# Block-causal attention with a SoLU feed-forward layer on one core: placing order by halves, loads shared by two pairs, W_out's rows permuted, and probabilities by way of DRAM for every second pair

## The chip, the cores and the metric

The kernel runs on one core of one Trainium2 chip, as one launch. The metric is the device time of that launch in microseconds (us). Before the change it is 729.7 us, the median of three runs (728.79 to 730.06).

A core has five engines with a program each. PE (TensorE) multiplies matrices, DVE (VectorE), ACT (ScalarE) and POOL (GpSimd) do elementwise work and reductions, and SP (SyncE) computes nothing: here it issues nearly all DMAs, one after the other. Each engine works through its own list of instructions in order. The DMAs themselves run on 16 DMA engines beside all of that.

## The reference

Eight batches of eight heads, 576 tokens, head size 64; then a feed-forward layer over all 4608 tokens:

```python
scores = scale * np.matmul(q, k.transpose(0, 1, 3, 2))      # scale = 1/8
mask = block_i >= block_j                                   # blocks of 64 tokens
attn = exp(scores - max) / (sum + 1e-09)
attn_out = np.matmul(attn, v)
x = attn_out.transpose(0, 2, 1, 3).reshape(4608, 512)
h = x @ w_in                                                # 512 -> 1024
sm = softmax(h); solu = h * sm
ln = (solu - mean) / sqrt(var + 1e-06) * g_ln
out = ln @ w_out                                            # 1024 -> 512
```

The weights w_in, w_out and g_ln arrive as 64-bit floats, q, k and v as 32-bit floats.

## The kernel before, in words

**Units of work.** Attention runs over 32 *pairs* p of heads (8 batches, 4 pairs each; heads 2hp and 2hp+1 in the two halves of the 128 partitions). The feed-forward layer, called MoE in the code, runs over 36 *tiles* t of 128 tokens. A tile can start when the four pairs of its batch are done. Products are made exact enough by splitting each operand in a high and a low part (names ending in h and l: `kh`, `kl`, `xh`, `xl`, `wih`, `wil`, `ch`, `cl`) and adding three matmul products.

**The order of the work** is not the order of the code. Every step is recorded by `op(engine, duration, function, ...)` with what it reads and writes, a key, and sometimes other engines that can do it (`alts`). `Schedule.run` (L109) then simulates all engines with these durations, always starting the ready step with the smallest key, and the instructions are issued in that order. The keys come from the table `PARAMS` (L41). An alternative engine is only open if its value there is under 3 (L79). A step of SP may have a `dma` time, which holds a simulated DMA channel, and a `tail` until its data have landed. At run time the engines keep this fixed order and wait for each other by semaphores.

**A pair** (function `attention`, L406). Pairs 0 to 3 transpose by PE; they are left out of what follows, as are the names with the ending 32.
1. `load` (L417) brings k and q into `kz` and `qz`: four DMAs each (L432), laid out so that DVE can transpose within blocks of 32 by 32. `loadv` (L439) brings v by three (L441, L445).
2. DVE transposes `kz` into `kt`, `qz` into `qt` (L474). ACT makes `kh`, `qh` (L475), POOL or DVE the low parts `kl` (L480, L481) and `ql` (L478). POOL casts the last 64 columns (L485).
3. PE computes the scores in PSUM (L515; the last block, L509). DVE masks and takes the row maximum (L536, L540); ACT takes the exponential into the probability buffer `pb` with row sums (L552).
4. DVE makes the reciprocals (L562, L563); POOL or ACT scales the probabilities (L570, L572). DVE transposes `pb` in place within blocks of 32 by 32 in two steps (L579).
5. `place` (L581) finishes the transposition by moving blocks between the quarters of the partitions: 16 DMAs, each 32 partitions of `pb` to 32 partitions of `pt` (L584):

```python
for r_ in range(4):
    for a_ in range(4):
        SP.dma_start(pt_[32 * r_ : 32 * r_ + 32, a_, :, :], pb[32 * a_ : 32 * a_ + 32, r_, :, :])
```

6. PE multiplies with v (`avmm`, L594: 52 matmul instructions at L596), ACT copies the result to `xt` (L395). `pb`, `pt` and `vr` have two buffers each; `kz`, `qz`, `kt`, `qt`, `kh` and the like have one.

**A tile** (function `moe`, L633). `xh` and `xl` (L648, L652), 24 matmuls with W_in (L673), row maximum (L679), exponential (L680), product (L681), then centring of `u` by the mean, on POOL or DVE (L683, L684), the square for the variance (L685). For tiles 4 to 34 (`PET <= t < PEL`) the centred tile is transposed by DVE into `zb` (L703), stored to a DRAM buffer `zd` (L704) and read back as `ct` (L705); ACT, POOL or DVE make `ch` (L711 to L713) and `cl` (L714, L715). Tiles 0 to 3 and 35 transpose by PE (L721, L724, L725). Then come 24 matmuls with W_out (L733), scaling (L737) and the store of the output (L739).

**Weights.** `prep` (L341) converts 16 pieces of weights at the start, one load each (L345), with `zb`, `ct` and `ob` as scratch space. L368 loads g.

Of the kernel before, what the change touches and what calls it, by code (L numbers as in the profile page):

```python
# [58 lines left out]
class Schedule:  # L59
# [49 lines left out]
    def run(self):  # L109
# [20 lines left out]
        while events:  # L130
# [18 lines left out]
            for e in engs:  # L149
# [46 lines left out]
                if best.dma > 0.0:  # L196
                    done = dmafree = max(done, dmafree) + best.dma
# [9 lines left out]
def kernel(  # L207
# [43 lines left out]
    qz, kz, qt, kt = (sb(x, [S]) for x in ("qz", "kz", "qt", "kt"))  # L251
# [87 lines left out]
    wkeys = []

    def prep(i, src, hi, lo, gcol, name, key):  # L341
# [3 lines left out]
        op("SP", 640, lambda: SP.dma_start(raw, src), w=[kr_], key=key, tail=2700, dma=1270)  # L345
# [60 lines left out]
    def attention(p):  # L406
# [7 lines left out]
        pep = p in PEP  # L414
        for nm, src, dst in (("kz", k, kz), ("qz", q, qz)):

            def load(nm=nm, src=src, dst=dst):  # L417
# [1 line left out]
                if peq:
                    for h in range(2):  # L420
                        dma.dma_start(
                            dst[:, 0:512].rearrange("p (c d) -> p c d", c=4)[:, :, 64 * h : 64 * h + 64],
                            src[b0, 2 * hp + h, 0:512, :].rearrange("(c p) d -> p c d", p=P),
                        )
                    r0 = 0 if nm == "kz" else 64
# [155 lines left out]
        def place():  # L581
            for r_ in range(4):
                for a_ in range(4):
                    SP.dma_start(pt_[32 * r_ : 32 * r_ + 32, a_, :, :], pb[32 * a_ : 32 * a_ + 32, r_, :, :])  # L584
# [199 lines left out]
```

## Time and profile before

| | |
|---|---|
| three runs | 728.79, 729.7, 730.06 us |
| profiled execution | 730.28 us |
| its span, first to last instruction | 728.5 us |
| mean granted clock of PE | 0.97 |
| moved by DMA | 125.49 MB, mean 172 GB/s |

The profile is of one execution. *Busy* is the time in which an engine has an instruction in work; PE's matmuls overlap, so a busy PE is not always at its peak. The stretches between busy times are idle, and a wait is put down to what ended it. In the profile's lines, "L596 PE MATMUL ps<-pt,vr" is line 596 of the kernel, the engine, the operation, and what it writes and reads; "SPq" is SP issuing a DMA, which is the time for issuing and not for moving data. The granted clock is 1.00 at full speed. The DMA share is the mean busy share of the 16 DMA engines.

### The profile page before, as it was taken

Reading aid. Unit: us, or ns where it says so; the run is one execution under the profiler, and the core shown is the slowest. Engines: PE = TensorE matmul, PEld = TensorE weight load, DVE = VectorE, ACT = ScalarE, POOL = GpSimd, SP = SyncE. Lnnn points to the kernel's source line nnn. Section 1 sums busy time; section 2 is a strip of 40 time slices with the busy share of each in tenths; the row PEclk is TensorE's granted clock in tenths of the full one; section 3 lists DMA queues with packets and bytes.
Section 4 is the critical chain, followed back from the end, with each engine's and each line's share of the span. In section 5 each row is a group of like instructions: output and inputs, shape, how many; then the busy total and the mean of one; then the engine's idle time right before and its main releaser. Section 6 shows DMA issues by size and latency. Waiting matters only on the chain.

```text
span 728.5 us, 14348 instructions
## 1 busy us (share of the span) xinstructions
PE 671.1 (92%) x4543; PEld 528.1 (72%) x4543; DVE 607.4 (83%) x1262; ACT 495.3 (68%) x1265; POOL 322.5 (44%) x491
## 2 busy tenths in 40 slices
PE   7786968999999998999999999899899988999997
PEld 6566757777677776778777777677677766878886
DVE  6999999988888999789799888899888789755672
ACT  5989958877777777665777686578585658434342
POOL 3755744454444655244353654245454434214310
PEclk7899989999999999999999999999999999999999
DMA  9584676676788888888778888888787874543431
GB/s 236 130 175 118 150 178 117 126 170 146 161 201 201 205 196 193 198 192 210 182 193 197 203 196 173 190 199 196 193 209 178 190 197 110 170 151 130 145 131 57
DMA packets 231547, 125.49 MB, mean 172 GB/s; under 512 B 190640, under 2 KB 206512, under 8 KB 231472
## 3 DMA queue, kind: packets, MB, share of 16 engines
q1 hardware_dynamic: 230416, 124.32, 70.1%
q8 instruction: 36, 0.59, 0.4%
q10 hardware_dynamic: 1056, 0.26, 0.2%
q14 instruction: 39, 0.32, 0.2%
HBM read 52.96 MB, written 25.69 MB: 108 GB/s over the span
## 4 chain that ended last, share of the span: by engine, by line
PE 32%; DVE 23%; SPq 14%; DMA 12%; ACT 12%; issue 5%; POOL 1%; DVEq 0%; ACTq 0%; POOLq 0%
PE ps L733 12%; SPq L584 11%; PE ps L673 9%; PE ps L596 5%; DVE pb L579 5%; DVE nm L540 5%; DMA pt<-pb 4%; ACT pb L552 4%; PE ps L515 4%; DMA ct<-zd 3%; ACT pb L572 3%; SPq L432 2%; DVE ub L681 2%; DVE zb L703 2%; PE ps L509 1%
## 5 line engine op out<-in xcount | busy, mean ns | idle before, releaser
L552 ACT ACTIVATE pb<-ps,nm 128x384 f32<-128x384 f32 (+4 forms) x288 | 157.3, 561 | 69.6 <-DVE nm L540 54.2
L540 DVE TENSOR_REDUCE nm<-ps 128x1 f32<-128x384 f32 (+4 forms) x288 | 131.8, 506 | 0.3
L596 PE MATMUL ps<-pt,vr 128*64 128x128 f32 (+2 forms) x1664 | 104.3, 286 | 25.4 <-DMA pt<-pb 13.7
L596 PEld LDWEIGHTS ps<-pt,vr 128*64 128x64 f32 x1664 | 90.2, 146 | 46.9 <-issue 16.4
L572 ACT ACTIVATE pb<-pb,rz 128x128 f32<-128x128 f32 (+4 forms) x191 | 101.2, 595 | 25.4 <-DVE rz L563 23.0
L579 DVE STREAM_TRANSPOSE pb<-pb 128x1536 f32<-128x1536 f32 (+1 forms) x56 | 102.1, 1829 | 9.5 <-POOL pb L570 5.8
L570 POOL TENSOR_SCALAR pb<-pb,rz 128x384 f32<-128x384 f32 (+4 forms) x97 | 62.3, 652 | 71.3 <-DVE rz L563 30.4
L733 PE MATMUL ps<-woh,ch 128*128 128x512 f32 x288 | 81.6, 405 | 4.0 <-ACT pb L552 3.4
L673 PE MATMUL ps<-wih,xh 128*128 128x512 f32 x288 | 83.8, 413 | 0.2 <-ACT xh L648 0.2
L673 PE MATMUL ps<-wil,xh 128*128 128x512 f32 x288 | 79.4, 398 | 0.0
L733 PE MATMUL ps<-woh,cl 128*128 128x512 f32 x288 | 78.7, 395 | 0.0
L673 PE MATMUL ps<-wih,xl 128*128 128x512 f32 x288 | 78.6, 395 | 0.0
L733 PE MATMUL ps<-wol,ch 128*128 128x512 f32 x288 | 78.6, 394 | 0.0
L733 PEld LDWEIGHTS ps<-woh,ch 128*128 128x128 f32 x288 | 51.8, 188 | 20.2 <-ACT pb L552 5.6
L703 DVE STREAM_TRANSPOSE zb<-ub 128x1024 f32<-128x1024 f32 x31 | 62.5, 2017 | 2.6 <-POOL ub L683 1.4
L673 PEld LDWEIGHTS ps<-wil,xh 128*128 128x128 f32 x288 | 54.8, 190 | 13.0
L673 PEld LDWEIGHTS ps<-wih,xh 128*128 128x128 f32 x288 | 51.1, 190 | 17.3 <-issue 4.8
L673 PEld LDWEIGHTS ps<-wih,xl 128*128 128x128 f32 x288 | 54.3, 188 | 12.8
L733 PEld LDWEIGHTS ps<-woh,cl 128*128 128x128 f32 x288 | 54.3, 188 | 12.8
L515 PE MATMUL ps<-kh,qh 64*128 64x384 f32 (+3 forms) x256 | 57.8, 390 | 6.2 <-ACT pb L552 1.8
L733 PEld LDWEIGHTS ps<-wol,ch 128*128 128x128 f32 x288 | 54.2, 188 | 12.7
L712 POOL TENSOR_SCALAR ch<-ct 128x512 fp32r<-128x512 f32 x36 | 22.0, 620 | 90.0 <-DMA ct<-zd 77.0
(116 smaller groups left out, 1262.3 us busy)
## 6 DMA issues: line engine op xcount, KB each, us to landing
pt<-pb SPq DMA_DIRECT2D x448, 100.0 KB, 2.2
zd<-zb SPq DMA_DIRECT2D x31, 512.0 KB, 3.0
ct<-zd SPq DMA_DIRECT2D x31, 512.0 KB, 4.3
out_dram<-ob SPq DMA_DIRECT2D x36, 256.0 KB, 3.1
vr<-in_v_dram SPq DMA_DIRECT2D x64, 128.0 KB, 3.3
kz<-in_k_dram SPq DMA_DIRECT2D x112, 72.0 KB, 2.7
qz<-in_q_dram SPq DMA_DIRECT2D x112, 72.0 KB, 3.0
ub<-in_moe_w_in_dram SPq DMA_DIRECT2D x8, 512.0 KB, 4.2
```

The costliest lines, as they stand in the source:

```text
L515: PE.matmul(PS(sps[h])[:, off : off + 128 * (i_ + 1)], w_[half[h], 128 * i_ : 128 * i_ + 128], x_[half[h], 0 : 128 * (i_ + 1)], start=n_ = ...
L540: op("DVE", t_dve(wid[u]), lambda sp=sp, off=off, u=u: DVE.tensor_reduce(out=nm_[u], in_=PS(sp)[:, off : off + wid[u]], axis=AX.X, op=ALU. ...
L552: ACT.activation(dst, src, AF.Exp, bias=nm_[u], accum_out=z_[zg][:, zc : zc + 1])
L570: op("POOL", 0.836 * nn + 243, lambda b=b, zg=zg, zc=zc: POOL.tensor_scalar(out=puv(pb, b, pep), in0=puv(pb, b, pep), scalar1=rz_[zg][:, z ...
L572: ("ACT", t_act(nn, 93), lambda b=b, zg=zg, zc=zc: ACT.activation(puv(pb, b, pep), puv(pb, b, pep), AF.Copy, scale=rz_[zg][:, zc : zc + 1] ...
L579: op("DVE", 1.058 * 128 * (s1 - s0) + 86, lambda s0=s0, s1=s1: DVE.transpose(pb[:, :, s0:s1, :], pb[:, :, s0:s1, :]), r=[("P", i, b) for b ...
L584: SP.dma_start(pt_[32 * r_ : 32 * r_ + 32, a_, :, :], pb[32 * a_ : 32 * a_ + 32, r_, :, :])
L596: PE.matmul(dst(PS(av)[half[h]]), vt[:, j, 64 * h : 64 * h + 64], pt_[:, a0:a1, sl, :], start=start, stop=stop)
L673: PE.matmul(o_, a_[:, c, :], w_[:, c, s_], start=(si == 0 and c == 0), stop=(si == 2 and c == NKI - 1))
L703: op("DVE", t_dve(DFF), lambda: DVE.transpose(zb.rearrange("p (r c i) -> p r c i", r=4, i=32), u.rearrange("p (c i r) -> p r c i", r=4, i= ...
L712: alts=[("POOL", 671, lambda c_=c_, h_=h_: POOL.tensor_scalar(out=h_, in0=c_, scalar1=1.0, scalar2=1.0, op0=ALU.mult, op1=ALU.mult), K["a_ ...
L733: PE.matmul(o_, a_[:, c, :], w_[:, c, :], start=(hf == 0 and si == 0 and c == 0), stop=(hf == 1 and si == 2 and c == 7))
```

## The change

**Pairs of heads.** A pair now holds heads ha and ha + 2, with `ha = 4 * (hp // 2) + zs` and `zs = p % 2`; the rows of W_in are loaded in the matching order, two DMAs a piece.

**Shared loads.** `kz` and `qz` get room for two pairs. From pair 4 on, every second pair issues four DMAs each for k and q that bring both pairs' data (`load2`). `kt` and `qt` are gone: DVE transposes in place, and the high and low parts read `kz` and `qz`.

**Placing.** For odd pairs the 16 DMAs go out in another order, by halves of the partitions. For pairs 4, 6, ..., 30 (`DRP`) one DMA stores the whole `pb` in a DRAM buffer `pd`, and four DMAs, after a wait for it, read `pt` from there.

**W_out's rows.** Row c\*128 + r\*32 + j of W_out (and of g) goes to partition 4j + r instead of 32r + j, by four DMAs a piece. L703 then reads 32 elements in a row where it read every fourth. Tiles 0 to 3 and 35, which transpose by PE, write the centred tile to `zb` in the permuted order; the first of them waits for all prepared weights, since `zb` is scratch space for these.

**Planner.** New durations for some steps, a DMA time of 5500 for `place` where it was 250, a limit on how far SP runs ahead of the DMAs (`DEPTH`), and a new table `PARAMS`. By it some alternatives close (centring on DVE, `ch` on POOL, `cl` on POOL, `xl` on DVE, scaling on ACT for pairs 0 to 3) and some open (the low part of the weights on POOL, the copies of kh and qh on DVE for pairs 0 to 3).

```diff
+DRP = tuple(range(4, 32, 2))
+PDMA = 5500
+DEPTH = 2500.0
-    "a_w": 189.2, "a_xh": -137.2, "a_xl": -269.8, "a_c": -179.5, "a_o": 359.2, "np": 32, "l0": -21.1,
+    "e1": 446.7, "e2": 16.2, "a_sp": 326.6, "a_sp32": 396.9, "a_lf": -295.5, "a_w": -763.6, "a_xh": 157.7,
+    "a_xl": 109.8, "a_c": 397.1, "a_o": 107.1, "np": 32, "l0": 36.7, "a_cl": -50.3, "a_ai": -221.8,
+    "aff": -308.3, "a_t3": -99.5, "a_cm": -493.3, "a_cg": 75.0, "a_sa": -235.7, "a_sa32": 555.4, "a_qh": 43.1,
+    "a_kl": -230.6, "a_ch": 260.5, "a_chd": 58.4, "a_clo": 184.7, "ct0": -293.1,
...
-                    done = dmafree = max(done, dmafree) + best.dma
+                    dmafree = max(t + min(best.dur, 600.0), dmafree) + best.dma
+                    engfree[e] = max(done, dmafree - DEPTH)
+                    done = max(engfree[e], dmafree)
...
-    qz, kz, qt, kt = (sb(x, [S]) for x in ("qz", "kz", "qt", "kt"))
+    qz, kz = (sb(x, [2, S]) for x in ("qz", "kz"))
+    pd = [dp.tile([P, 4, NSL * 32], F32, name=f"pd{i}") for i in range(2)]
...
-    w_in_w = w_in.bitcast(U32).rearrange("(c p) (n t) -> p c n t", p=P, t=2)
-    w_out_w = w_out.bitcast(U32).rearrange("(c p) (n t) -> p c n t", p=P, t=2)
+    w_in_w = w_in.bitcast(U32).rearrange("(a h z d) (n t) -> d a z h n t", h=2, z=2, d=64, t=2)
+    w_out_w = w_out.bitcast(U32).rearrange("(c r j) (n t) -> r j c n t", r=4, j=32, t=2)
+    def rows(dst, src):
+        for r_ in range(4):
+            SP.dma_start(dst[r_::4], src[r_])
+    def heads(dst, src):
+        for h in range(2):
+            SP.dma_start(dst[64 * h : 64 * h + 64], src[:, h])
...
+        zs = p % 2
+        ha = 4 * (hp // 2) + zs
+            def load2(nm=nm, src=src, dst=dst):
+                for g in range(4):
+                    SP.dma_start(
+                        dst[32 * g : 32 * g + 32].rearrange("p m (g d) -> p (m g) d", d=32),
+                        src[b0, ha + g - g % 2 : ha + g - g % 2 + 2, :, 32 * (g % 2) : 32 * (g % 2) + 32].rearrange("m (g p) d -> p (m g) d", p=32),
+                    )
+            elif zs == 0:
+                op("SP", 2600, load2, w=[(nm, 0), (nm, 1)], key=lk, tail=1700, dma=3740)
...
-            op("DVE", t_dve(S) + 30, lambda z=z, t=t: DVE.transpose(t, z), r=[x + "z"], w=[x + "t"], key=kk)
+            op("DVE", t_dve(S) + 30, lambda z=z: DVE.transpose(z, z), r=[zk], w=[zk], key=kk)
...
-            for r_ in range(4):
-                for a_ in range(4):
+            for d_ in (2, 3, 0, 1):
+                for a_ in (0, 2, 1, 3):
+                    r_ = a_ ^ d_
                     SP.dma_start(pt_[32 * r_ : 32 * r_ + 32, a_, :, :], pb[32 * a_ : 32 * a_ + 32, r_, :, :])
+        if p in DRP:
+            def back():
+                for r_ in range(4):
+                    SP.dma_start(pt_[32 * r_ : 32 * r_ + 32, :, :, :].rearrange("p a s i -> p a (s i)"), pd_[:, r_, :].rearrange("(a p) n -> p a n", a=4))
+            op("SP", 630, lambda: SP.dma_start(pd_, pb.rearrange("p r s i -> p r (s i)")), r=tk, w=[("pd", p % 2)], key=p + K["pe" + sfx], tail=1700, dma=4000)
+            op("SP", 4 * 560, back, r=[("pd", p % 2)], w=ptk, key=p + K["pe" + sfx], tail=1700, dma=4000)
+        elif not pep:
+            op("SP", 16 * 633, place, r=tk, w=ptk, key=p + K["pe" + sfx], tail=1500, dma=PDMA)
...
+        if not PET <= t < PEL:
+            dst, src = (x.rearrange("p (c a b) -> p c a b", a=a_, b=P // a_) for x, a_ in ((zb, 32), (u, 4)))
+            src = src.rearrange("p c r j -> p c j r")
+            cw, ck = ["zb"], "zb"
...
-            op("DVE", t_dve(DFF), lambda: DVE.transpose(zb.rearrange("p (r c i) -> p r c i", r=4, i=32), u.rearrange("p (c i r) -> p r c i", r=4, i=32)), r=[uk] + (wkeys if t == PET else []), w=["zb"], key=key + K["ct"])
+            op("DVE", t_dve(DFF), lambda: DVE.transpose(zb.rearrange("p (r c i) -> p r c i", r=4, i=32), u.rearrange("p (c r i) -> p r c i", r=4, i=32)), r=[uk] + (wkeys if t == PET else []), w=["zb"], key=key + K["ct"])
```

More of the change, by code (lines that the diff above doesn't have):

```diff
@@ L344, in prep @@
         kr_, k1, k2, k3 = ("ub", i % 2), ("w1", i % 2), ("w2", i % 2), ("ob", i % 2)
-        op("SP", 640, lambda: SP.dma_start(raw, src), w=[kr_], key=key, tail=2700, dma=1270)
+        if gcol is None:
+            op("SP", 2 * 640, lambda: heads(raw, src), w=[kr_], key=key, tail=2700, dma=1270)
+        else:
+            op("SP", 4 * 640, lambda: rows(raw, src), w=[kr_], key=key, tail=2700, dma=1270)
         high = raw[:, :, 1].bitcast(F32)
@@ L414, in attention, with load @@
         pep = p in PEP
+        zs = p % 2
+        ha = 4 * (hp // 2) + zs
         for nm, src, dst in (("kz", k, kz), ("qz", q, qz)):
-            def load(nm=nm, src=src, dst=dst):
+            def load(nm=nm, src=src, dst=dst[:, zs]):
                 dma = ACT if p == 0 and nm == "kz" else SP
[L419 to L425, printed above, removed]
+                for h in range(2):
+                    dma.dma_start(
+                        dst[:, 0:512].rearrange("p (c d) -> p c d", c=4)[:, :, 64 * h : 64 * h + 64],
+                        src[b0, ha + 2 * h, 0:512, :].rearrange("(c p) d -> p c d", p=P),
+                    )
+                r0 = 0 if nm == "kz" else 64
+                SP.dma_start(
+                    kq[r0 : r0 + 64, :].rearrange("p (h d) -> p h d", h=2),
+                    src[b0, ha : ha + 3 : 2, 512:576, :].rearrange("h p d -> p h d"),
+                )
+            def load2(nm=nm, src=src, dst=dst):
+                for g in range(4):
@@ L472, in attention @@
                 op("DVE", t_dve(q1 - q0), lambda q0=q0, q1=q1, ps_=ps_, o_=o_: DVE.scalar_tensor_tensor(out=ql_[:, q0:q1], in0=PS(ps_)[:, q0 + o_ : q1 + o_], scalar=0.125, in1=qh_[:, q0:q1].bitcast(F32), op0=ALU.mult, op1=ALU.subtract), r=[k_], w=[("ql", iq, 0) if q0 == 0 else ("ql", iq)], key=ke, ps=ps_)
[L473 to L476 removed]
+        for x, z, hi, lo, scale in () if peq else (("k", kz[:, zs], kh_, kl_, 1.0), ("q", qz[:, zs], qh_, ql_, 0.125)):
+            zk = (x + "z", zs)
+            op("DVE", t_dve(S) + 30, lambda z=z: DVE.transpose(z, z), r=[zk], w=[zk], key=kk)
+            op("ACT", t_act(S), lambda z=z, hi=hi, scale=scale: ACT.activation(hi, z, AF.Copy, scale=scale), r=[zk], w=[(x + "h", iq)], key=ke,
+               alts=[("POOL", 0.836 * S + 243, lambda z=z, hi=hi, scale=scale: POOL.tensor_scalar(out=hi, in0=z, scalar1=scale, scalar2=1.0, op0=ALU.mult, op1=ALU.mult), K["a_qh"])])
@@ L521, in attention @@
             else:
-                d, md = sum(3 * t_row(128 * (i_ + 1)) for i_, _ in us) + {1: 0, 2: 48, 3: 74}[us[0][0]], 2
+                d, md = sum(3 * t_row(128 * (i_ + 1)) for i_, _ in us) + {1: 90, 2: 48, 3: 74}[us[0][0]], 2
                 rd = [(x, iq) for x in ("kh", "kl", "qh", "ql")] + [(x, iq, 0) for x in ("qh", "ql")]
```

58 lines of the change are left out of this document (24 added, 34 removed), and 11 rows, old and new, of the table PARAMS.

## The prediction

> **What bounds the kernel now.** I read the page first, then busy time by stage, what TensorE (PE) waited for, and last SP's queue in order of time. PE does 36 MoE tiles and 32 head pairs of work whatever the schedule, so I ask where it sits idle and why.
>
> ```profile
> span 728.5 us, 14348 instructions
> ...
> PE 671.1 (92%) x4543; PEld 528.1 (72%) x4543; DVE 607.4 (83%) x1262; ACT 495.3 (68%) x1265; POOL 322.5 (44%) x491
> ...
> PE 32%; DVE 23%; SPq 14%; DMA 12%; ACT 12%; issue 5%; POOL 1%; DVEq 0%; ACTq 0%; POOLq 0%
> ```
>
> PE is idle for 728.5 - 671.1 = 57.4 us; no schedule of the same matmuls can win much more. The chain that ended last is spread over all engines, with 26% in SP's queue and DMAs. By stage (columns: length, then PE, PEld, DVE, ACT and POOL busy, PE clock, DMA share, GB/s):
>
> ```profile
> 0.00:120.00 120.00, 93.63 (x737) 73.63 (x738) 106.83 (x253) 99.08 (x266) 67.31 (x108) 0.87 0.70 162
> 120.00:620.00 500.00, 473.47 (x3281) 370.51 (x3280) 436.77 (x908) 354.32 (x923) 231.21 (x349) 0.99 0.78 184
> 620.00:728.50 108.50, 103.97 (x529) 83.92 (x527) 63.81 (x103) 41.89 (x77) 23.99 (x35) 1.00 0.39 130
> ```
>
> The start loses 26.4 us with DVE busy 89% of it (weight preparation beside four pairs). The middle, 28 pairs at steady pace, loses 26.5. The end, MoE tiles alone, loses 4.5. In the middle the largest cause is this (us, times, longest), with one such wait and one undisturbed block of the same 52 matmuls, and the granted clock (next to last but two) during the late block:
>
> ```profile
> PE ps L596 <- DMA pt<-pb: 13.7, 7, 4.3
> ```
> ```profile
> 289.32 4.57 PE L596 MATMUL ps<-pt,vr 128*64 128x128 f32 x52 [2.52 <-DMA pt<-pb]
> ```
> ```profile
> 309.08 2.98 PE L596 MATMUL ps<-pt,vr 128*64 128x128 f32 x52
> ```
> ```profile
> 289.30:293.90 4.60, 4.58 (x53) 3.88 (x53) 2.95 (x3) 0.49 (x1) 0.00 (x0) 0.64 0.94 223
> ```
>
> Half of the middle's idle time is the probability-times-V block (L596) waiting for the placing DMAs (L584). A wait costs twice: the 52 matmuls behind it take 4.57 us instead of 2.98, at a clock of 0.64. Seven waits are 13.7 us plus up to 7 x 1.59 = 11.1 us. By the Trainium skill (TensorE: Matmul & The Clock Gate, Part 1: The HAM clock gate) the clock halves after an idle window of about 3.4 us; the trace shows the slow block behind a gap of 2.52 us already. By the page's figure only one or two of seven waits, 2.0 us long on average, would be followed by a slow block, and the sum below would be some 5 us smaller, 717. Why the placing is late shows in SP's queue (start, duration):
>
> ```profile
> 237.34 10.57 SPq L584 DMA_DIRECT2D pt<-pb  x16
> 248.01 0.53 SPq L704 DMA_DIRECT2D zd<-zb  x1
> 248.64 1.30 SPq L441 DMA_DIRECT2D vr<-in_v_dram  x2
> 249.99 0.71 SPq L445 DMA_DIRECT2D vr<-in_v_dram  x1
> 250.75 2.23 SPq L432 DMA_DIRECT2D kz<-in_k_dram  x4
> 253.08 0.44 SPq L705 DMA_DIRECT2D ct<-zd  x1
> 253.62 3.21 SPq L432 DMA_DIRECT2D qz<-in_q_dram  x4
> 256.92 1.02 SPq L441 DMA_DIRECT2D vr<-in_v_dram  x2
> 257.99 0.65 SPq L445 DMA_DIRECT2D vr<-in_v_dram  x1
> 258.73 10.69 SPq L584 DMA_DIRECT2D pt<-pb  x16
> ```
> ```profile
> L584 SPq DMA_DIRECT2D pt<-pb x448: 507/591/2012, 88.4 to 639.5; - x150
> ```
>
> From one placing to the next, 21.39 us, SP issues for 20.66 us (97%): it is full. The 28 placings span 639.5 - 88.4 = 551 us, 19.7 us a pair, and a pair's own issues sum to it: 10.6 placing + 5.4 for k and q + 1.7 for v + about 1.5 for its MoE tile's three = 19.2 us. So SP's issue time sets the pace of attention in the middle, and whatever is queued behind 16 placings waits 10.6 us.
>
> **Part 1, SP's issues.** For 14 of the 28 pairs, 16 issues become one store of the whole buffer and four read-backs. A store is priced as L704's row (0.53), a read-back by L705's 0.44 to L432's 0.56 apiece: 2.3 to 2.8 us, 2.7 taken, saving 7.9. Shared loads issue four DMAs a tensor for two pairs instead of eight: half of 2 x 5.4, saving 5.4 per two pairs. Two pairs fall from 38.4 to 25 us of SP, from full to about 65% of today's pace. Direct placing and the load of the next pairs can then start when their data are ready.
>
> What else is on the way once SP is free: the latency of placing, and the DMA engines.
>
> ```profile
> pt<-pb SPq DMA_DIRECT2D x448, 100.0 KB, 2.2
> zd<-zb SPq DMA_DIRECT2D x31, 512.0 KB, 3.0
> ct<-zd SPq DMA_DIRECT2D x31, 512.0 KB, 4.3
> ```
>
> Direct: 10.6 us of issue + 2.2 to land = 12.8 us. By DRAM no row shows 1600 KB. Lower bound: 3.0 us for the store, as if size were free, + 1.8 of issue + 4.3 = 9.1 us. Upper bound: both landings scaled by size, 3.1 x 3.0 + 1.8 + 3.1 x 4.3 = 24 us. A fixed part is plainly in 100 KB's 2.2 us, so about 0.8 us per 412 KB (3.0 - 2.2): the store lands in 5.1 us and the read-back, whose four parts overlap its issue, some 5 to 6 after the last: 13 us, the direct route's latency. The read-back makes SP wait for the store; behind it stand loads and the MoE tile's zd and ct, which the new plan places in that gap, so I charge nothing but keep 5 us per pair in mind.
>
> DMA load, from two stretches, one inside 16 placings issued alone, one led by the store to zd of 248.01 (columns as above):
>
> ```profile
> 276.44 11.07 SPq L584 DMA_DIRECT2D pt<-pb  x16
> ```
> ```profile
> 284.00:286.00 2.00, 2.00 (x11) 1.61 (x10) 1.97 (x5) 2.00 (x8) 1.76 (x5) 1.00 0.70 158
> ```
> ```profile
> 248.00:250.00 2.00, 1.44 (x7) 0.82 (x5) 0.58 (x4) 2.00 (x6) 1.92 (x4) 1.00 0.86 278
> ```
>
> Per full share that is 226 GB/s between buffers on the chip and 323 GB/s to DRAM. A pair's 1.64 MB costs 7.3 us of all engines directly. By DRAM the store costs 5.1; the read-back costs 5.1 at the store's rate or 7.3 at the placing's, since it too writes 32 partitions at a time. That adds 2.9 to 5.1 us per pair, 40 to 71 us on 0.78 x 500 = 390, a share of 0.86 to 0.92 at today's pace. The order by halves, which lets successive placings start from other quarters of the partitions and always end in the other half for the first eight, can bring the direct 7.3 down to the store's 5.1 at best and to nothing at worst; issue at 10.6 us hides either. I take no gain from it. The Trainium skill (SBUF — State Buffer, "Can I just issue two DMAs to hit both halves?") speaks against it: two concurrent transfers at partitions 0 and 64 gave 6% over one. By that 7.3 would become 6.9, and the sum stays. DMA gets fuller but has room; I charge +4 us for longer queues.
>
> Gain in the middle: of the seven waits I take two thirds as gone, 9 us idle and 7 us slow clock, since half of the pairs still issue 16 placings. Of the other 12.8 us idle, part follows from the same pace: 4 us. Sum -20.
>
> **Part 2, W_out's rows permuted.** It makes L703's source contiguous runs of 32 instead of steps of four.
>
> ```profile
> L703 DVE STREAM_TRANSPOSE zb<-ub 128x1024 f32<-128x1024 f32 x31 | 62.5, 2017 | 2.6 <-POOL ub L683 1.4 <-DMA zd<-zb 0.8
> ```
> ```profile
> L579 DVE STREAM_TRANSPOSE pb<-pb 128x1536 f32<-128x1536 f32 x28 | 49.3, 1761 | 6.3 <-POOL pb L570 5.8 <-ACT pb L572 0.2 <-DMA pt<-pb 0.2
> ```
> ```profile
> L714 DVE TENSOR_TENSOR cl<-ct,ch 128x512 fp32r<-128x512 f32 x27 | 21.1, 802 | 10.8 <-ACT ch L711 10.2 <-PE ps L733 0.6
> ```
> ```profile
> L683 POOL TENSOR_SCALAR ub<-ub,ms 128x1024 f32<-128x1024 f32 x11 | 12.4, 1123 | 22.6 <-DVE ms L682 12.3 <-DVE ms L688 10.0
> L684 DVE TENSOR_SCALAR ub<-ub,ms 128x1024 f32<-128x1024 f32 x25 | 20.0, 800 | 0.6
> ```
>
> L579 with contiguous runs takes 1761/1536 = 1.15 ns an element, so L703 falls to about 1.17 us: 31 x 0.84 = 26 us of DVE. The new parameters also close some choices: a_c over 3 sends L684's 25 centrings to POOL (20 us off DVE, 28 on POOL), and a_clo over 3 sends all `cl` to DVE (35 x 0.80 = 28 us on). DVE ends some 18 us lighter of 607. It waits for nothing in the middle that bounds PE, so I count 1 us.
>
> The price: tiles 0 to 3 and 35 centre into zb in permuted order, reading runs with a step of 32. The bound below is 1.12 us as now; above, the factor of L703 against L579, 2017/1174 = 1.7, gives 1.9 us. Four of them are in the start, and the first waits there for all prepared weights, which its W_out matmuls (L733) wait for anyway; one is in the last chain, where other matmuls run until near the end. I charge 1 us to the end.
>
> **The start** gets 35 more DMA issues (four instead of one for each of eight W_out loads, two for each of eight W_in loads, four for g), about 35 x 0.6 = 21 us of SP. Their cover is SP's slack there:
>
> ```profile
> 56.52 0.34 SPq L345 DMA_DIRECT2D ub<-in_moe_w_out_dram  x1
> 65.70 0.92 SPq L441 DMA_DIRECT2D vr<-in_v_dram  x2
> ```
>
> That gap alone is 8.8 us. Without it, each load would come up to 2 us later, 16 x 2 = 32 us. DVE bounds this stage and gets less to do; the two placings that hold SP from 88.4 on shrink. I charge -2.
>
> **Sum:** -20 (middle) + 4 (DMA) - 1 (DVE) + 1 (end) - 2 (start) = -18. The profiled execution took 730.28 us (1.8 beside its span), the median is 729.7; 730.3 - 18 = 712.3, less 0.6 for the median, so **712 us**. All waits and slow blocks gone, with the other idle of the middle: 730 - 26.5 - 11 = 692; I put the likeliest case's own range at 699 to 723.
>
> **Rivals.** (a) *The DMA engines take SP's place.* The Trainium skill (DMA: Bandwidth & Descriptors, Issuing engines are not separate DMA queues) calls issue time small beside the transfer; by that, saving issues gains nothing. For it: the share is 0.78 already, and 40 to 71 us are added. Against: SP at 97% with 0.70 in a stretch of pure placing. If the waits for `pt` and the slow blocks stay, the sum keeps -4 + 4 - 1 + 1 - 2 = -2: 728; if every DRAM pair waits another 0.5 us, 735. (b) *PE has little to regain*: the freed gaps come back as waits for ACT and DVE, since PE is at 95%: half of 20 is lost, 722. (c) *The shared load is late* (slower). With the copies kt and qt gone, k and q stay in their buffer until `kl` and `ql` are made, so the next two pairs load only after that:
>
> ```profile
> 315.95 0.76 DVE L478 SCALAR_TENSOR_TENSOR ql<-qt,qh 128x576 fp32r<-128x576 f32 x1 [0.81 <-ACT qh L475]
> ```
> ```profile
> 328.78 1.44 POOL L481 TENSOR_TENSOR kl<-kt,kh 128x576 fp32r<-128x576 f32 x1 [0.94 <-ACT kh L475]
> ```
>
> From 316.7 to the next pair's transposition, some 1.5 us before 328.8, there are 10.6 us. Issue (2.2) and landing (about 4, as ct) take 6.2 for k; q, behind it, 8.4. It fits unless SP is in a direct placing (10.6 us) at that moment: then it is some 6 us late. If that happens at 14 loads with half of it reaching PE, 14 x 3 = 42 against -18: 754; it decides against the change from 1.3 us a load. (d) *The new order does nothing and the bounce runs no better*: 728 to 730.
>
> **Numbers.** Forecast 0.62, (a) 0.17, (b) 0.09, (c) 0.08, (d) 0.04. About 0.2% is what a measurement here can tell, 1.5 us. Faster: 0.62 + 0.09 + 0.08 of (a) = 0.79. Same: 0.04 of (a) + 0.03 of (d) = 0.07. Slower: 0.08 + 0.05 of (a) + 0.01 of (d) = 0.14. The range, 696 to 729, takes in (b) and the better half of (a); it leaves out (c), most of (d), the worse part of (a) and what lies under 696.
>
> **What would show it.** SP's queue with gaps in the middle and five issues instead of 16 for every second pair; PE's wait for `pt` under 7 us; L703 near 1.17 us; PE's idle in the middle under 15 us; DMA share 0.82 to 0.92. I am wrong if PE's wait on DMA keeps its 13.7 us (a), if `kt`'s transposition waits for loads by over 1.3 us at each of 14 places (c), or if PE's idle grows in the first 120 us.

## The result and the profile after

The changed kernel takes 775.1 us (773.6 to 775.3, four runs) against 729.75 for the kernel before on the same chip: a ratio of 1.062, interval 1.0601 to 1.0638. It is 45 us slower, where 712 was forecast and the range ended at 729. The prediction was wrong in sign. Ratios compare fast executions only; one of x14's ten (736.7 us) and one of x16's four (1241.4 us, the profiled one, hence x19) were slow and are left out.

In this kernel's lines the exponential is L575, the transposition of `pb` L602, the direct placing L608, the store to DRAM L619, the read-back L617, P·V L630, the transposition of a tile L743, its store L744 and its read-back L745. First the page: span, busy times, and the chain that ended last, by engine.

```profile
span 773.5 us, 14040 instructions
...
PE 690.3 (89%) x4543; PEld 544.0 (70%) x4543; DVE 575.8 (74%) x1260; ACT 509.2 (66%) x1282; POOL 303.5 (39%) x476
...
PE 43%; DMA 23%; DVE 18%; ACT 5%; SPq 4%; issue 4%; POOL 3%; DVEq 0%; POOLq 0%; ACTq 0%
```

SP's queue has left the chain (14% to 4%), as forecast, and the DMAs have taken its place (12% to 23%). By stage (columns as in the prediction):

```profile
0.00:120.00 120.00, 93.08 (x661) 73.07 (x663) 104.08 (x249) 95.08 (x246) 70.43 (x109) 0.90 0.76 164
120.00:620.00 500.00, 453.03 (x3103) 355.54 (x3099) 392.35 (x854) 342.49 (x885) 194.46 (x312) 0.94 0.92 215
620.00:773.50 153.50, 144.15 (x786) 115.35 (x786) 79.32 (x157) 71.61 (x151) 38.61 (x55) 0.98 0.45 139
```

PE is idle for 47.0 us of the middle where it was idle for 26.5, its clock there is 0.94 where it was 0.99, and the DMA share is 0.92 where it was 0.78. After 620 us, 786 matmuls are left where 529 were: the loss is made in the middle and only paid at the end. What PE waits for, and the P·V group of both kernels, before first:

```profile
PE ps L630 <- DMA pt<-pd: 44.4, 11, 4.5
```
```profile
L596 PE MATMUL ps<-pt,vr 128*64 128x128 f32 (+2 forms) x1664 | 104.3, 286 | 25.4 <-DMA pt<-pb 13.7 <-ACT pb L552 6.7 <-ACT woh L362 2.7
```
```profile
L630 PE MATMUL ps<-pt,vr 128*64 128x128 f32 (+2 forms) x1664 | 121.9, 314 | 54.3 <-DMA pt<-pd 44.4 <-DMA out_dram<-ob 5.0 <-DMA pt<-pb 2.7
```

The wait for `pt` has not shrunk from 13.7 us; it has grown to 44.4 under the name of the read-back, at 11 of the 14 DRAM pairs. The same 1664 matmuls take 121.9 - 104.3 = 17.6 us longer: most blocks behind these waits run at a low clock. 44.4 - 13.7 + 17.6 = 48 us, about the whole loss. Now one DRAM pair, in SP's queue and on PE (start, duration, and in brackets the idle time before):

```profile
215.61 0.46 SPq L619 DMA_DIRECT2D pd<-pb  x1
216.52 9.08 SPq L450 DMA_DIRECT2D qz<-in_q_dram  x4
225.70 0.62 SPq L744 DMA_DIRECT2D zd<-zb  x1
226.42 1.29 SPq L463 DMA_DIRECT2D vr<-in_v_dram  x2
227.76 0.69 SPq L467 DMA_DIRECT2D vr<-in_v_dram  x1
228.55 0.54 SPq L779 DMA_DIRECT2D out_dram<-ob  x1
229.13 1.87 SPq L617 DMA_DIRECT2D pt<-pd  x4
```
```profile
240.44 5.60 PE L630 MATMUL ps<-pt,vr 128*64 128x128 f32 x52 [4.49 <-DMA pt<-pd]
252.52 2.98 PE L630 MATMUL ps<-pt,vr 128*64 128x128 f32 x52
```

From the store's issue to PE's start there are 24.8 us, where the prediction had 13. This store lands after 9.6 us, at 225.2. The read-back is issued 4 us later, since SP is busy with loads, four of which take 9.08 us to issue behind the store. Five of the 14 pairs have such a gap of 4 to 4.6 us between the store's landing and the read-back. At the other nine the read-back goes out within 0.8 us of the landing, and PE starts late as well, 16.3 to 19.6 us after the store's issue. Here the store lands 6.1 us after its issue:

```profile
349.18 0.55 SPq L619 DMA_DIRECT2D pd<-pb  x1
355.32 1.75 SPq L617 DMA_DIRECT2D pt<-pd  x4
```
```profile
366.43 4.28 PE L630 MATMUL ps<-pt,vr 128*64 128x128 f32 x52 [4.50 <-DMA pt<-pd]
```

What all pairs share is the read-back itself (columns: issues, KB each, median us from issue to landing):

```profile
pd<-pb SPq DMA_DIRECT2D x14, 1600.0 KB, 6.2
pt<-pd SPq DMA_DIRECT2D x56, 400.0 KB, 7.4
pt<-pb SPq DMA_DIRECT2D x224, 100.0 KB, 2.6
```

The four quarters of a pair, 400 KB to 32 partitions each, land one after the other, 2.0 us apart (median), and the last lands 9.7 us after its issue (median of the 14 pairs, 8.6 to 10.8). From the store's issue to that landing it is 18.2 us in the median pair.

### The profile page after: what moved, and what is told of

Its sections match the earlier page's. It is cut to its first block, busy times and chain, and to the rows that moved or that the text cites. A ratio compares the mean times of both kernels' runs of the same rounds, so it can differ in the third digit from the quotient of the medians.

```text
span 773.5 us, 14040 instructions
## 1 busy us (share of the span) xinstructions
PE 690.3 (89%) x4543; PEld 544.0 (70%) x4543; DVE 575.8 (74%) x1260; ACT 509.2 (66%) x1282; POOL 303.5 (39%) x476
## 3 DMA queue, kind: packets, MB, share of 16 engines
q1 hardware_dynamic: 228512, 147.24, 79.8%
## 4 chain that ended last, share of the span: by engine, by line
PE 43%; DMA 23%; DVE 18%; ACT 5%; SPq 4%; issue 4%; POOL 3%; DVEq 0%; POOLq 0%; ACTq 0%
PE ps L707 13%; DMA pt<-pd 12%; PE ps L773 12%; PE ps L630 11%; PE ps L538 4%; DVE pb L602 4%; DMA pd<-pb 4%; DVE nm L563 4%; ACT pb L575 2%; SPq L617 2%; POOL pb L593 2%; DMA ct<-zd 2%; DVE ms L713 1%; PE ps L532 1%; ACT pb L595 1%
## 5 line engine op out<-in xcount | busy, mean ns | idle before, releaser
L575 ACT ACTIVATE pb<-ps,nm 128x384 f32<-128x384 f32 (+4 forms) x288 | 157.1, 561 | 29.5 <-DVE nm L563 28.6
L630 PE MATMUL ps<-pt,vr 128*64 128x128 f32 (+2 forms) x1664 | 121.9, 314 | 54.3 <-DMA pt<-pd 44.4
L630 PEld LDWEIGHTS ps<-pt,vr 128*64 128x64 f32 x1664 | 103.8, 163 | 78.9 <-issue 54.6
L593 POOL TENSOR_SCALAR pb<-pb,rz 128x384 f32<-128x384 f32 (+4 forms) x137 | 84.4, 630 | 95.0 <-ACT pb L575 60.8
L602 DVE STREAM_TRANSPOSE pb<-pb 128x1536 f32<-128x1536 f32 (+1 forms) x56 | 102.0, 1829 | 5.8 <-POOL pb L593 4.1
L754 DVE TENSOR_TENSOR cl<-ct,ch 128x512 fp32r<-128x512 f32 x62 | 43.9, 712 | 72.0 <-ACT ch L751 68.9
L751 ACT ACTIVATE ch<-ct 128x512 fp32r<-128x512 f32 x62 | 37.1, 626 | 89.8 <-DMA ct<-zd 85.0
L722 POOL TENSOR_SCALAR ub<-ub,ms 128x1024 f32<-128x1024 f32 x31 | 34.9, 1126 | 131.5 <-DVE ms L716 85.8
L595 ACT ACTIVATE pb<-pb,rz 128x384 f32<-128x384 f32 (+4 forms) x151 | 78.8, 593 | 11.0 <-DVE rz L586 10.2
```

The costliest lines, as they stand in the source:

```text
L575: ACT.activation(dst, src, AF.Exp, bias=nm_[u], accum_out=z_[zg][:, zc : zc + 1])
L593: op("POOL", 0.836 * nn + 243, lambda b=b, zg=zg, zc=zc: POOL.tensor_scalar(out=puv(pb, b, pep), in0=puv(pb, b, pep), scalar1=rz_[zg][:, z ...
L595: ("ACT", t_act(nn, 133), lambda b=b, zg=zg, zc=zc: ACT.activation(puv(pb, b, pep), puv(pb, b, pep), AF.Copy, scale=rz_[zg][:, zc : zc + 1 ...
L602: op("DVE", 1.058 * 128 * (s1 - s0) + 86, lambda s0=s0, s1=s1: DVE.transpose(pb[:, :, s0:s1, :], pb[:, :, s0:s1, :]), r=[("P", i, b) for b ...
L630: PE.matmul(dst(PS(av)[half[h]]), vt[:, j, 64 * h : 64 * h + 64], pt_[:, a0:a1, sl, :], start=start, stop=stop)
L722: op("POOL", 1097, lambda: POOL.tensor_scalar(out=dst, in0=src, scalar1=m[:, 3:4], scalar2=1.0, op0=ALU.add, op1=ALU.mult), r=[uk, ("m3", ...
```

## The experiments

The **theory** after the result: the SP argument holds, and the read-back into quarters of 32 partitions makes it worthless. **Rivals:** SP was never the bound (the DMA engines are); the new order of work is worse whatever the route; the shared loads are at fault. Each ratio is to the kernel before on the same chip (its medians: 730.75 to 732.6 us).

### The route alone, in the changed order

`x1_direct_same_plan` issues eight direct placings where the store stood and eight where the read-backs stood; all engines keep the changed kernel's order.

```diff
-SP.dma_start(pd_, pb...)                     # store
+place((2, 3))
-for r_ in range(4): SP.dma_start(pt_[32 * r_ : 32 * r_ + 32, ...], pd_[:, r_, :]...)
+place((0, 1))
```

> The changed kernel, its order on every engine kept, but pairs 4, 6, ..., 30 place directly: eight of the 16 placings stand where the store stood, eight where the read-backs stood. Theory A (the way by DRAM is too slow: PE waits 44.4 us for pt<-pd and its blocks behind run at a slow clock): these waits go, SP gets 7.9 us more per such pair, so 720 to 738 us. Theory B (the new table's order of work is worse by itself): 760 to 775. Theory C (the shared loads and the fuller DMA queue hold everything up): 755 to 775, as the bytes by DRAM are only a part of it.

732.1 us, 1.0013 (0.9989 to 1.0037). In this order the other parts of the change cost nothing together, and gain nothing; the whole loss of 6% is the trip by DRAM. `x2_direct_replanned` has the direct route too (`DRP = ()`) and lets the planner order the work anew with the same table.

> The changed kernel with no pair by way of DRAM; the planner orders the work anew with 16 placings for each pair. Theory A: as the kernel before or better, since loads still cost SP less and L743 is faster: 712 to 730 us. Theory B: 755 or more. Theory C: 750 or more, with waits for kz and qz.

786.3 us, 1.0752 (1.0709 to 1.0795). Route and work are those of x1, so the 54 us between them are the order: from the same table, with the direct route, the planner makes a bad one. Which step of it is bad was not followed up. `x4_before_dram` gives the order before the store and the four read-backs, for every second pair, in place of 16 placings.

> The kernel before with its order kept; only the placing of pairs 4, 6, ..., 30 becomes one store and four read-backs behind it, on the spot, with SP waiting for the store in between. Theory A: 14 pairs become late by some 4 to 5 us and PE's blocks behind them slow: 750 to 790 us. Theories B and C: SP issues 5 instead of 16 and the time stays or falls, 720 to 735.

784.4 us, 1.0738 (1.0693 to 1.0782): SP stands 88.7 us waiting for stores and PE 40.9 for read-backs. Without a new order the trip is dearer still.

### What makes the read-back slow

`x3_read_back_128` reads back in one DMA to all 128 partitions, `x5_read_back_quarters` in four of 400 KB, each to all 128 partitions, `x6_read_back_alternating` in the four of the change, in the order 0, 2, 1, 3. x3 and x5 leave out the exchange of blocks between the quarters.

```diff
-for r_ in range(4): SP.dma_start(pt_[32 * r_ : 32 * r_ + 32, ...], pd_[:, r_, :]...)
+SP.dma_start(pt_..., pd_)                                                # x3
+for a_ in range(4): SP.dma_start(pt_[:, a_, :, :]..., pd_[:, a_, :])     # x5
+for r_ in (0, 2, 1, 3): ...                                              # x6
```

> The changed kernel with its order kept, but the four read-backs of 32 partitions each are one of 128 partitions that brings every row back to its own partition: the placing between partitions is left out for the 14 pairs. Theory A1 (the read-back is slow because each of its DMAs writes 32 partitions): 1600 KB land in about 6 us as the store does, PE's wait for pt falls by some 3 to 4 us per pair, 735 to 755 us. Theory A2 (the read-back is late because of the wait for the store and what stands between the two on SP): 765 to 775. Theories B and C: 770 to 776.

> The changed kernel with its order kept; the read-back is still four DMAs of 400 KB in rows of 3200 bytes, but each goes to all 128 partitions (one quarter of the columns); the placing between partitions is left out for the 14 pairs, as in x3. Theory P (a DMA that writes only 32 partitions moves its data more slowly): as x3, 728 to 738 us. Theory N (four DMAs, or rows of 3200 instead of 12800 bytes, are what is slow): as the changed kernel, 760 to 778.

> The changed kernel with its order kept; only the four read-backs go out for quarters 0, 2, 1, 3 of the partitions instead of 0, 1, 2, 3, so that successive ones write different halves. Theory P with halves that can be written at the same time: part of the loss returns, 740 to 765 us. Theory P with DMAs that are served one after the other, and theory N: 770 to 778.

732.4 us (1.0012, 0.9991 to 1.0034), 732.6 (1.0023, 1.0 to 1.0046) and 769.3 (1.0513, 1.0471 to 1.0555). The read-back and PE's wait, of x3 and then of x5:

```profile
pt<-pd SPq DMA_DIRECT2D x14, 1600.0 KB, 7.5
```
```profile
PE ps L629 <- DMA pt<-pd: 15.1, 10, 3.3
```
```profile
pt<-pd SPq DMA_DIRECT2D x56, 400.0 KB, 5.1
```
```profile
PE ps L630 <- DMA pt<-pd: 11.3, 9, 2.7
```
```profile
L630 PE MATMUL ps<-pt,vr 128*64 128x128 f32 (+2 forms) x1664 | 103.2, 283 | 22.7 <-DMA pt<-pd 11.3 <-DMA out_dram<-ob 4.0 <-ACT pb L595 2.4
```

x5 has the changed kernel's count, bytes, route and place in SP's queue; only the partitions that one DMA writes are other. That takes the landing from 7.4 us to 5.1, the wait from 44.4 to 11.3, the matmuls from 121.9 to 103.2, and nearly all of the loss away. Its quarters land 1.1 us apart, the last 6.5 us after its issue and 14.6 after the store's (medians). The same five pairs have about 4 us between the store's landing and the read-back, so that gap is not what costs the 6%.

The quarters also keep the DMA engines at work for longer: the transfers that SP issues take 79.8% of the 16 engines' 773.5 us in the changed kernel, 617 us, and 78.4% of 730.0 in x5, 572 us. Fuller engines alone do not make the loss, since in x14 below it is 82.9% of 727.0, 603 us, without it; how much of it they add is not shown.

x3 came out better than the 735 to 755 expected. x6 fell between its two ranges; its mixed halves give back about 1% of the 6%.

`x8_read_back_one` does the whole computation with this. For the DRAM pairs the exponential reads the scores in steps of four keys, so that one DMA of 128 partitions brings every block to its place:

```diff
-src.rearrange("p (c r i) -> p c r i", r=4, i=32)
+src.rearrange("p (c i r) -> p c r i" if p in DRP else "p (c r i) -> p c r i", r=4, i=32)
...
-for r_ in range(4): SP.dma_start(pt_[32 * r_ : 32 * r_ + 32, ...], pd_[:, r_, :]...)
+SP.dma_start(pt_.rearrange("p a s i -> p a (s i)"), pd_.rearrange("(a p) r n -> (p r) a n", a=4))
```

> The changed kernel with its order kept, whole computation: in the 14 pairs by DRAM the exponential writes its keys in such an order (every fourth to a block) that one DMA of 128 partitions brings all of pt back in place; it reads PSUM in steps of four elements for that. Theory P: as x3, 728 to 738 us, if ACT reads steps of four at full rate; with the factor 1.7 that L703 paid for them, 126 exponentials of 0.56 us get 50 us more on ACT, and 738 to 760. Theory N: below the changed kernel too, since it is one DMA; it does not tell P from N, x5 does.

727.8 us, 0.9959 (0.9938 to 0.998): faster than both kernels, but by 0.4% and not by 2.5%. `x14_dram_all_pairs` sends all 28 pairs that way, with a table made for it.

> As x8, but all 28 pairs from pair 4 on go by DRAM with one store and one read-back, and a table found for that with the planner, so order and route differ from x8. SP issues 2 instead of 16 for each placing. Theory S: 700 to 718 us. Theory D (28 x 1.64 MB more than direct, the DMA engines above 0.9): 728 to 760.

728.2 us, 0.9949 (0.9925 to 0.9974). Twice as many issues saved, and no gain over x8; the share of the DMA engines in the middle is 0.95. The middle of x8 and of x14:

```profile
120.00:620.00 500.00, 479.32 (x3400) 375.54 (x3399) 422.23 (x919) 369.92 (x959) 207.69 (x334) 0.99 0.90 234
```
```profile
120.00:620.00 500.00, 475.37 (x3344) 371.27 (x3343) 450.34 (x1000) 331.52 (x863) 221.63 (x361) 0.99 0.95 272
```

### Was SP's issue time the bound at all?

Three kernels with the order before: `x11_before_half_placing` leaves out eight of each 16 placings, `x12_eight_issues_all_bytes` moves all bytes by eight of 200 KB, `x13_half_bytes` keeps 16 issues and moves 12 of 25 slices.

```diff
-for a_ in range(4): SP.dma_start(pt_[32*r_:32*r_+32, a_, :, :], pb[32*a_:32*a_+32, r_, :, :])
+for a_ in (r_, r_ ^ 2): ...                                                     # x11
+for a_ in (0, 2): SP.dma_start(pt_[32*r_:32*r_+32, a_ : a_ + 2, ...], ...)      # x12
+SP.dma_start(pt_[32*r_:32*r_+32, a_, 0:12, :], pb[32*a_:32*a_+32, r_, 0:12, :]) # x13
```

> The kernel before with its order kept, with only 8 of the 16 placings of each of 28 pairs: half of the placing is left out. SP gets 5.3 us of 19.2 less per pair, more than the change takes. If SP's issue time sets the pace of the kernel (the prediction's step): the seven waits for pt and their slow blocks go, 705 to 716 us. If it only seems to, since PE has its work from MoE tiles meanwhile: 722 to 731.

> The kernel before with its order kept; 8 placings of 200 KB instead of 16 of 100 KB per pair, all bytes moved, but not all to the right place. If SP's issues set the pace (theory S): as x11, 705 to 714 us. If the bytes on the DMA engines do (theory D): 722 to 731. If both limits lie close together: in between, 714 to 722.

> The kernel before with its order kept; all 16 placings per pair, but each moves 12 of the 25 slices, so 48% of the bytes; the rest of the placing is left out. Theory S: SP stays full, 725 to 731 us. Theory D: 705 to 715. Both close together: 715 to 725.

708.7 us (0.9673, 0.9613 to 0.9733), 708.8 (0.9695, 0.9663 to 0.9726) and 725.9 (0.9922, 0.9892 to 0.9952). The middle of x12, then of x13:

```profile
120.00:620.00 500.00, 489.85 (x3411) 382.27 (x3410) 451.12 (x934) 360.48 (x942) 237.21 (x354) 1.00 0.83 192
```
```profile
120.00:620.00 500.00, 477.43 (x3298) 373.13 (x3297) 441.33 (x917) 355.16 (x928) 231.07 (x349) 0.99 0.58 143
```

Half of the issues with all bytes gain 3.05%, all issues with 48% of the bytes 0.8%. The median issue of a placing takes the same time at 200 KB (x12) and at 48 KB (x13) as at 100 KB before, 591 ns (shortest, median and longest in ns, then the first and last start):

```profile
L585 SPq DMA_DIRECT2D pt<-pb x224: 507/590/1149, 89.6 to 614.1; - x112
```
```profile
L584 SPq DMA_DIRECT2D pt<-pb x448: 507/589/1801, 89.4 to 634.8; - x150
```

So SP's issue time was the bound, as the prediction read it from the queue; PE's wait for `pt` is gone from x12, and PE is busy 489.85 of 500 us at full clock. The rival that the DMA engines are the bound of the kernel before falls.

Can the issues go to another engine? `x16_half_from_pool` and `x17_half_from_act` keep order and bytes and give eight of every pair's 16 placings, those that read the upper half of `pb`'s partitions, to GpSimd or to ScalarE; `x19_half_from_pool_again` is x16 once more, for its profile.

```diff
-SP.dma_start(pt_[32 * r_ : 32 * r_ + 32, a_, :, :], ...)
+(POOL if a_ > 1 else SP).dma_start(...)     # x16, x19; ACT in x17
```

> The kernel before with all of its work; of each pair's 16 placing DMAs the eight of the second half are issued by GpSimd instead of SyncE. Theory S (SyncE's issue time sets the pace of the middle, its bytes do not): SyncE loses the same 224 issues as in x12, so the time goes most of the way to x12's 708.8 us: 709 to 722. Rival P (the issue time only moves: GpSimd must wait at each pair for the exps and the transposes that it copies from, and what is queued behind them, its share of the transposes pb, kl and qdl, comes late): 728 to 760, with PE's waits now on tiles that GpSimd makes.

> As x16, but the eight are issued by ScalarE. Theory S: 709 to 722. Rival P: ScalarE is 68% busy and its next exps stand behind the eight issues and the wait for the pair's last transposes; if that decides, 728 to 760, and PE waits for pb or kh where it waited for pt. Between the two engines, the one whose queue holds less behind the issue should be the faster.

> The same kernel as x16, for a profile: 735 to 745 us, SyncE waiting little, and PE's or VectorE's waits on GpSimd's tiles longer than in the kernel before, since GpSimd stands at each pair's eight issues until the last transposition.

x16 has a ratio of 1.0106 (1.0042 to 1.017), x19 took 738.6 us, x17 829.1 (1.1324, 1.1278 to 1.1369). By the times the rival held for x16, and x17 is far above even its 760 us. GpSimd's wait for the transposition before its placings in x19; then ScalarE's idle time that ends with its placings in x17, eight of these in its queue, and the copy behind them:

```profile
POOL pt L584 <- DVE pb L579: 16.5, 5, 7.0
```
```profile
ACT pb L552 <- DMA pt<-pb: 59.3, 10, 9.0
```
```profile
308.67 5.02 ACTq L584 DMA_DIRECT2D pt<-pb  x8
313.74 1.09 ACT L395 ACTIVATE xt<-ps 128x384 f32<-128x384 f32 x4 [4.91 <-DVE zb L703]
```

In that stretch ScalarE, which makes the next scores' exponentials, spends 5 us on eight issues. How x16 loses is open: in x19 PE's wait for `pt` falls from 13.7 to 2.7 us, its longest wait on a tile of GpSimd is 4.3 us, once, and SyncE, expected to wait little, waits for more than before (315 us in all against 180).

### The other parts, alone

Each in the order before: `x7_before_halves` the order of the 16 placings, `x9_before_shared` the loads of two pairs (k and q in the new grouping of heads, v and W_in in the old one, so the result is another and the work the same), `x10_before_transpose` the contiguous source of L703 (W_out's rows stay, so the result no longer matches them).

```diff
+for d_ in (2, 3, 0, 1): for a_ in (0, 2, 1, 3): r_ = a_ ^ d_; ...             # x7
+if p % 2: return                                                              # x9
+SP.dma_start(dst2[32*g : 32*g + 32]..., src[b0, 2*hp+g-g%2 : 2*hp+g-g%2+2, ...])
-u.rearrange("p (c i r) -> p r c i", r=4, i=32)                                # x10
+u.rearrange("p (c r i) -> p r c i", r=4, i=32)
```

> The kernel before with its order kept; only the 16 placings of each pair go out in the order by halves. If a DMA's 32 partitions limit it and the halves can work at the same time, placings under load land sooner, and PE's wait for pt (13.7 us) falls: 720 to 727 us. If SP's issue of 0.6 us each is what sets the pace: 727 to 732, no change.

> The kernel before with its order kept; every second pair loads k and q for itself and the next by four DMAs each, the other pairs issue none (kt and qt kept, kz and qz with room for two pairs; the heads are those of the new grouping while v and W_in keep the old one, so which keys meet which values is changed, and the work is the same). If SP's issues set the pace (the prediction's step): 2.7 us of 19.2 less per pair, attention runs ahead, 718 to 726 us. If the matmuls set the pace: 727 to 732. If the shared load is late (rival c): over 735.

> The kernel before with its order kept; only L703 reads runs of 32 instead of every fourth element, with W_out's rows left as they were, so the matching of the two is left out. 31 x 0.84 = 26 us less on DVE. By the prediction this is worth 1 us: 727 to 731. If DVE is what the middle waits for: 715 to 725.

731.1 us (0.9989, 0.9968 to 1.0011), 740.7 (1.0122, 1.009 to 1.0154) and 727.7 (0.9947, 0.9921 to 0.9973). The order by halves does nothing. The shared loads cost 1.2% in the order before. SP's load issues, before and then in x9 (ns: shortest, median, longest; first and last start):

```profile
L432 SPq DMA_DIRECT2D kz<-in_k_dram x112: 312/496/1868, 37.5 to 579.7; - x112
L432 SPq DMA_DIRECT2D qz<-in_q_dram x112: 312/496/1827, 40.1 to 596.0; - x112
```
```profile
L437 SPq DMA_DIRECT2D kz<-in_k_dram x56: 332/711/2200, 39.0 to 585.8; - x56
L437 SPq DMA_DIRECT2D qz<-in_q_dram x56: 378/843/2941, 42.8 to 591.6; - x56
```

Half as many issues, each 1.4 to 1.7 times as long (medians). And DVE's transpositions wait more for them: 8.1 us for `qz` and 5.2 for `kz` in x9, where it was 1.4 and 3.0 before. In the changed order of x1 the same loads cost nothing that shows.

### The change without the second trip

`x20_two_issues_all_bytes` is the changed kernel in its own order; the store and the read-backs become two direct DMAs of half the tile.

```diff
-SP.dma_start(pd_, pb...)                     # store
+SP.dma_start(pt_[:, 0:2, :, :], pb[:, 0:2, :, :])
-for r_ in range(4): SP.dma_start(pt_[32 * r_ : 32 * r_ + 32, ...], pd_[:, r_, :]...)
+SP.dma_start(pt_[:, 2:4, :, :], pb[:, 2:4, :, :])
```

> The changed kernel with its own order on every engine, but every second pair's probabilities go straight from pb to pt in two DMAs of 800 KB, half of the tile each, where the 128-partition store and the read-backs stood; they land on the partitions that they come from, so the blocks are not exchanged: all bytes of a direct placing, 2 issues for 16, and none of DRAM's second trip. If the bytes of the second trip are what keeps the mended DRAM way (x8, 727.8 us) from SyncE's gain, this one gets it: 705 to 716. If the order and the shared loads keep it, it stays at 724 to 732.

714.8 us, 0.9743 (0.9685 to 0.9801). Its middle, its P·V group and its DMAs:

```profile
120.00:620.00 500.00, 488.03 (x3495) 381.76 (x3494) 423.48 (x928) 375.43 (x970) 212.08 (x338) 1.00 0.81 194
```
```profile
L629 PE MATMUL ps<-pt,vr 128*64 128x128 f32 (+2 forms) x1664 | 98.8, 277 | 6.3 <-ACT kh L498 2.2 <-ACT pb L575 1.5 <-ACT pb L595 1.1
```
```profile
pt<-pb SPq DMA_DIRECT2D x28, 800.0 KB, 4.9
```

PE no longer waits for `pt`. Against x8, which has nearly the same issues in the same order, the second trip costs 0.9959 - 0.9743 = 0.022, about 16 us. On PE this is what x8 still waits for read-backs, and the slower matmuls behind:

```profile
L629 PE MATMUL ps<-pt,vr 128*64 128x128 f32 (+2 forms) x1664 | 101.9, 282 | 17.6 <-DMA pt<-pd 12.9 <-ACT pb L595 2.2 <-ACT pb L575 1.5
```

12.9 us of waits and 101.9 - 98.8 = 3.1 us of matmuls come to the same 16 us. The four DMAs into quarters cost 1.062 - 0.9959 = 0.066 more, about 48 us, of which x5 puts 44 on the partitions. What makes the second trip cost is open. x20 does not tell its bytes (DMA share 0.90 in x8, 0.81 here) from its latency, nor from SP's standing still for the store before the read-back, 23.4 us in x8 at nine pairs and 56.3 in x14 at 19. x14 cannot tell them apart either, since its order is another one.

## Why the prediction was wrong, step by step

- **The bound (right).** SP's queue was full, and its issue time set the pace: x12 gains 22 us with all bytes moved. Without its charge for DMA the sum was -22; x20, with two issues for those pairs where the change has five, measures -2.57%, 19 us. The gain was there to be had.
- **"By DRAM: 13 us, the direct route's latency" (the step that failed).** The store was sized about right, 6.2 us to landing for 5.1. The read-back was not: "some 5 to 6 after the last" issue is 9.7 us, because its four parts land 2.0 us apart. So `pt` is complete 18.2 us after the store's issue in the median pair and not after 13, and PE waits, some 4 us at 11 of the 14 pairs. The new order of work had no room for this: the planner's own durations for the two steps, 0.6 + 4.0 + 1.7 us each, come to 12.6. With all 128 partitions per DMA (x5) it is 14.6, and nearly all of the loss is gone. The bounds of the same paragraph, 9.1 and 24 us, held this; the choice between them did not.
- **The queue between store and read-back (noted, charged nothing).** It delays five of the pairs by about 4 us, such as the one with 24.8 us above. It does so in x5 too, where the loss is gone, so it did not decide.
- **"It too writes 32 partitions at a time" (noted, and not followed).** The sentence used it only for the DMA engines' load, 7.3 us for 5.1. It belonged to the latency as well, which is on PE's path: x5 is the same read-back with other partitions, and PE's wait falls from 44.4 to 11.3 us. The load was also above its range: SP's transfers take 617 us of the engines against 536 (73.6% of 728.6) in x1, 5.8 us more per pair where 2.9 to 5.1 was the estimate.
- **"+4 for longer queues" (mis-sized).** It was the sum's only charge for the route by DRAM, which measures 64 us against x20: 16 for the trip as in x8, 48 for the quarters.
- **"Two thirds of the waits gone" (reversed).** Late blocks also ran at a lower clock, as the prediction said. Of the 11 late blocks ten take 4.28 to 5.60 us where 2.98 is the undisturbed time; with the sign of the wait wrong, the same effect worked against the forecast. Its size before was read too high: of the seven waits only three, of 2.52, 4.35 and 3.01 us, have a slow block behind them (4.57, 4.62 and 4.34 us), 4.6 us in all and not up to 11.1, so the 7 us counted for the clock are more than these blocks had to give.
- **The shared loads, "saving 5.4 per two pairs" (wrong).** The issue of a shared load was priced like that of a single one, and takes 1.4 to 1.7 times as long in x9. Bytes alone hardly explain it, since placings of 48, 100 and 200 KB issue in the same 0.59 us and x8's read-back of 1600 KB in 0.37; the cause stays open. Four loads of q took 3.21 us before and 9.08 behind the store, 6.1 of them one issue. In the order before the shared loads alone cost 1.2%.
- **W_out's rows (right in size, undercounted in worth).** The transposition takes 1.23 us for 1.17, and x10 gains 0.5% by it, some 4 us where 1 was counted. The permuted centring takes 2.18 us, above the bound of 1.9; five of them were too few to matter.

```profile
L743 DVE STREAM_TRANSPOSE zb<-ub 128x1024 f32<-128x1024 f32 x31 | 38.1, 1230 | 12.5 <-POOL ub L722 10.4 <-DMA zd<-zb 2.1
L722 POOL TENSOR_SCALAR zb<-ub,ms 128x1024 f32<-128x1024 f32 x5 | 10.9, 2179 | 13.6 <-DVE ms L716 8.2 <-PE ps L761 3.2 <-issue 2.2
```

- **The start (-2).** It stayed at 26.9 us of idle PE against 26.4: neither the extra issues nor the lighter DVE show.
- **The halves (no gain taken, right).** The Trainium skill (SBUF — State Buffer, "Can I just issue two DMAs to hit both halves?") gives 6% for two concurrent transfers; x7 shows nothing, and in x6 mixing the read-backs' halves recovers about 1%.
- **The rivals.** (c) did not come: DVE's transpositions hardly wait for loads in the changed kernel. (a), the DMA engines in SP's place, had 728 as its time, and x8 (727.8, with 12.9 us of PE's waits on read-backs) and x14 (728.2) come out there; whether the DMA engines are the reason is not shown. No rival had the mechanism that came: a latency on PE's path, repeated at 11 of 14 pairs.

## What to carry to other kernels

When a step is moved to another route to save issues, follow one item from its producer to its consumer, and sum what it takes until the last of its parts has landed; a route that is cheap to issue can be late. On a path that something waits for, try a DMA that covers all 128 partitions, even if the data must be laid out otherwise upstream. And take the price of an issue from a row of the same shape of DMA with the same things queued ahead of it, not from its bytes.

## What the runs showed of the hardware

- In a series of four, 400 KB from DRAM land in 7.4 us in 32 partitions, 2.0 us apart, and in 5.1 in 128 partitions, 1.1 us apart (x5; medians); 1600 KB in one DMA of 128 partitions land in 7.5 (x3).
- SyncE issues a placing in 0.59 us, be it of 48, 100 or 200 KB (x13, before, x12; medians).
- ScalarE reads PSUM in steps of four keys at the full rate. The exponentials of the kernel before, then of x8, 14 of whose 32 pairs read so:

```profile
L552 ACT ACTIVATE pb<-ps,nm 128x384 f32<-128x384 f32 (+4 forms) x288 | 157.3, 561 | 69.6 <-DVE nm L540 54.2
```
```profile
L575 ACT ACTIVATE pb<-ps,nm 128x384 f32<-128x384 f32 (+4 forms) x288 | 157.0, 561 | 25.1 <-DVE nm L563 21.9
```

- The length of the gap alone does not settle the clock. In x8 a gap of 2.70 us is followed by a slow block, in the changed kernel one of 3.39 is not:

```profile
463.94 4.39 PE L629 MATMUL ps<-pt,vr 128*64 128x128 f32 x52 [2.70 <-DMA pt<-pd]
```
```profile
654.39 2.98 PE L630 MATMUL ps<-pt,vr 128*64 128x128 f32 x52 [3.39 <-DMA pt<-pd]
```

In the traces the granted clock changes only at steps of 3.41 us (in the changed kernel every stretch at half clock is 3.4, 6.8 or 10.2 us long, but for the one that its end cuts off). So where the gap falls counts too. The gap of x8 lies mostly within one step, and PE is busy for 1.21 of its 3.41 us; the other one falls across a step, and PE is busy for 1.98 and 1.46 us of the two (columns as in the prediction; x8, then the changed kernel):

```profile
460.04:463.45 3.41, 1.21 (x6) 0.64 (x4) 0.68 (x6) 0.00 (x0) 1.12 (x1) 1.00 1.01 318
463.45:466.86 3.41, 2.92 (x20) 2.16 (x22) 0.28 (x1) 0.94 (x2) 0.00 (x0) 0.50 0.57 149
```
```profile
649.02:652.43 3.41, 1.98 (x9) 1.27 (x7) 3.38 (x6) 3.09 (x8) 0.58 (x2) 1.00 1.05 215
652.43:655.85 3.42, 1.46 (x19) 1.32 (x21) 2.71 (x4) 2.09 (x4) 2.18 (x4) 1.00 0.66 196
```
